# Top-32 attention with two expert layers on one core: where a step's reciprocal, two-slope pass, bias and scaling stand among the weight conversion's parts, and the order of the first loads

## The chip, the cores and the metric

The kernel runs as one program on one core of a Trainium2 chip. The metric is the device time of one execution in microseconds (us); for a set of runs it is the median. An engine works through its own queue in order, and waits on semaphores of other engines or of DMA transfers. PE is the matrix engine (PEld its weight loads), DVE the vector engine, ACT the scalar engine, POOL the general one (GpSimd), and SP the queue that issues the DMA transfers.

## What is computed

```python
scores = scale * np.matmul(q, k.transpose(0, 1, 3, 2))      # 4 batches, 8 heads, 576 x 576
kth = np.partition(scores, -32, axis=-1)[..., -32:-31]
scores = np.where(scores >= kth, scores, -1e9)
attn = np.exp(scores - scores.max(-1, keepdims=True))
attn = attn / (attn.sum(-1, keepdims=True) + 1e-9)
x = np.matmul(attn, v)                                       # regrouped to 2304 tokens x 512
h = (x @ w1) * (x @ w2) @ w3                                 # 512 -> 1024 -> 1024
x = h @ w_out                                                # 1024 -> 512
# then eight experts: P from x @ w_gate by exp and eight rounds of row and column scaling
out = sum(P[:, e:e + 1] * (np.maximum(x @ w1e[e], 0) @ w2e[e]) for e in range(8))
```

All inputs and outputs are float32. The change touches the attention alone, and beside it the conversion of the weights `w_out`, `w3`, `w1` and `w2`.

## The kernel before, in words

**Steps.** The attention is cut into 72 steps. A step `s` takes two tiles of 128 query rows against 576 keys, for two heads of one pair `p` (a pair lasts four and a half steps). The work of one step is spread over several passes of the loop at line 610. In pass `s` the program issues:

- `st_topk(s)` on DVE: the 32 largest of each row by four rounds of MAX8 (line 220) with MATCH_REPLACE8 between (line 226), for both tiles; it fills `tkv`.
- `st_rec(s - 2)` on DVE: the reciprocal of the row sums `rden` (line 254), between the two first MAX8 of `st_topk(s)`.
- `st_over(s - 1)` on ACT, twice: the two-slope pass over `s_sb` with the 32nd value from `tkv` (line 233). `st_bias(s - 1)` on POOL: `nbias` from `tkv` (line 238).
- `st_norm(s - 2)` on POOL, twice: `e_sb` times the reciprocal (line 260).
- `st_scores(s + 1, 0)` and later `(s + 1, 1)`: four matmuls (line 197) and ACT's copy to `s_sb` (line 201).
- `st_exp(s - 1, 0)` and later `(s - 1, 1)` on ACT: the exponential with `nbias` (line 245), which adds up `rden`; behind the second, `eps` is added to `rden` (line 248).
- `st_trans(s - 2, 0)` and `(s - 2, 1)`: PE transposes `e_sb` (line 266), ACT copies to `et` (line 269); then `st_av(s - 2)`: PE times `v` (line 299) and ACT's copy to `xT` (line 303).

The program is written in this order and stands so in each engine's queue; there is no scheduler. Between these parts stand pieces of a pair's preparation (`prep_split`, `prep_group`, `prep_swap`: `k` and `q` are split in two parts, transposed by PE, and the transposed `k` in `kst0` is copied with its halves exchanged to `kst1` by DMA, line 158) and matmuls that were put on a list to be filled in (`run_fill`).

**The weight conversion.** In passes 0 to 21 forty blocks of 128 x 512 weights are converted as well. `cv_run` issues ACT's part at the end of a pass: two activations (lines 350 and 351, which write `ca` in `G` and `cb`), and a third (355) for blocks of `w_out`. DVE's parts, `c1` (358), `c2` (362) and `c3` (372), wait on a list, `dve_q`; `st_topk` of the next pass takes one from it behind each pair of MAX8 and each pair of MATCH_REPLACE8 (`dve_slot`), so seven times a step. `c3` also issues POOL's addition (line 375, or 377 for `w1` and `w2`, for `w_out` with 370 ahead of it) and the load of a later block (323, on SP's queue). For `w1` and `w2`, ACT's rounding (333) and POOL's remainder (334) follow at `cv_flush`. A step with two blocks thus has 13 instructions of the search and up to six parts of the conversion on DVE.

Since `st_bias` and `st_norm` are called behind `st_topk`, they stand in POOL's queue behind the additions that `st_topk` has issued through `dve_slot`.

**The first loads.** Ahead of the loop, lines 573 to 594 load the first pair's `k`, `q` and `v`, the first block of `w_out`, split and transpose `k` and `q`, load the second pair's `k` and `q`, two more blocks, the second pair's `v`, exchange the halves of `kst` by two transfers of 288 KB, and issue the first scores.

Behind the attention (from about 925 us) stands the expert part, whose code the change doesn't touch.

Of the kernel before, what the change touches and what calls it, by code (L numbers as in the profile page):

```python
# [7 lines left out]
F32 = mybir.dt.float32  # L8
F32R = mybir.dt.float32r
U16 = mybir.dt.uint16  # L10
U32 = mybir.dt.uint32
AF = mybir.ActivationFunctionType
# [5 lines left out]
def kernel(  # L18
# [14 lines left out]
    nc = tc.nc  # L33
    B, H, S, D = q.shape
# [10 lines left out]
    S4 = R * 128  # L45
# [26 lines left out]
    ap1 = att.enter_context(tc.tile_pool(name="att", bufs=1, side="right"))  # L72
# [21 lines left out]
    def load_pair(p):  # L94
        b, hp = divmod(p, HP)
        for nm, src in (("k", k), ("q", q)):
            t = ap1.tile([128, 2 * R + 1, D], F32, name=f"{nm}n", tag=f"{nm}n", bufs=1)
            nc.sync.dma_start(
                t[:, 0:2 * R].rearrange("p (h r) d -> p h (r d)", h=2),
                src[b, 2 * hp:2 * hp + 2, 0:S4, :].rearrange("h (p r) d -> p h (r d)", r=R))  # L100
            for i in range(2):
                nc.sync.dma_start(t[64 * i:64 * i + 64, 2 * R], src[b, 2 * hp + i, S4:S, :])
            nat[nm, p] = t

    def load_v(p):
        b, hp = divmod(p, HP)
        t = vn_t[p % 2]
        for i in range(2):
            nc.sync.dma_start(t[:, R * i:R * i + R, 0:D],
                              v[b, 2 * hp + i, 0:S4, :].rearrange("(p r) d -> p r d", r=R))  # L110
        for i in range(2):
            nc.sync.dma_start(t[64:128, 2 * R + i, 0:D], v[b, 2 * hp + i, S4:S, :])

    kst = {}
    split = {}

    def copy(dst, src, eng):
        if eng is None:
            nc.scalar.activation(dst, src, AF.Copy)
        else:  # L120
            eng.tensor_copy(dst, src)

    def prep_split(p, nm, eng=nc.gpsimd):
        src = nat.pop((nm, p))
        hl = ap1.tile([128, 2 * R + 1, 2, D], F32R, name=f"{nm}hl", tag=f"{nm}hl")
        nc.scalar.activation(hl[:, :, 0, :], src, AF.Copy)
        eng.tensor_tensor(hl[:, :, 1, :], src, hl[:, :, 0, :].bitcast(F32), ALU.subtract)
        split[nm, p] = hl

    def prep_group(p, nm, g, eng=None):  # L130

        hl = split[nm, p]
        pt = mps.tile([128, 512], F32, name="pt", tag="mm")
        chunks = list(range(R * g, R * g + R)) if g < 2 else [2 * R]
        for j, c in enumerate(chunks):
            src = hl[:, c].rearrange("p a d -> p (a d)")
            nc.tensor.transpose(pt[:, 128 * j:128 * j + 128], src.bitcast(F32), ident)  # L137
        if nm == "q":
            dst = qst_t[p % 2]
            if g < 2:  # L140
                copy(dst[:, S4 * g:S4 * g + S4], pt, eng)
            else:
                copy(dst[:, 2 * S4:2 * S4 + 64], pt[:, 0:64], eng)
                copy(dst[:, 2 * S4 + 192:2 * S4 + 256], pt[:, 64:128], eng)
        else:
            if (p, 0) not in kst:
                kst[p, 0] = ap1.tile([128, 2, S], F32R, name="kst0", tag="kst0", bufs=2)
            dst = kst[p, 0]
            if g < 2:
                copy(dst[:, g, 0:S4], pt, eng)  # L150
            else:
                copy(dst[:, :, S4:S], pt[:, 0:128].rearrange("p (h r) -> p h r", h=2), eng)

    def prep_swap(p):

        kst[p, 1] = ap1.tile([128, 2, S], F32R, name="kst1", tag="kst1", bufs=2)
        for i in range(2):
            nc.sync.dma_start(kst[p, 1][64 * i:64 * i + 64].bitcast(F32),
                              kst[p, 0][64 - 64 * i:128 - 64 * i].bitcast(F32))

    def prep_list(p):
        ops = [lambda: prep_split(p, "k"), lambda: prep_split(p, "q")]
# [19 lines left out]
    eps = const.tile([128, 1], F32, name="eps")  # L182
# [23 lines left out]
    def dve_slot(n=1):  # L206
        for _ in range(n):
            if dve_q:
                fn = dve_q.pop(0)
                if fn is not None:  # L210
                    fn()

    def st_topk(st, between):

        s = [s_sb[st][:, j] for j in range(2)]
        a = [ap1.tile([128, S], F32, name=f"tk{j}", tag=f"tk{j}") for j in range(2)]
        vt = ap1.tile([128, 2, TOPK], F32, name="tkv", tag="tkv", bufs=3)
        for r in range(TOPK // 8):
            for j in range(2):
                nc.vector.max(vt[:, j, 8 * r:8 * r + 8], a[j] if r else s[j])  # L220
                if between:
                    between.pop(0)()
            dve_slot()
            if r < TOPK // 8 - 1:
                for j in range(2):
                    nc.vector.match_replace(a[j], vt[:, j, 8 * r:8 * r + 8], a[j] if r else s[j], -3.0e38)  # L226
                dve_slot()
        tkv[st] = vt

    def st_over(st, j):  # L230

        x = s_sb[st][:, j]
        nc.scalar.activation(x, x, AF.Prelu, bias=tkv[st][:, j, TOPK - 1:TOPK], scale=-1.0, alpha=2.0 ** -100)

    def st_bias(st):
        nbias[st] = ap1.tile([128, 2], F32, name="nbias", tag="nbias", bufs=2)
        vt = tkv.pop(st)
        nc.gpsimd.tensor_tensor(nbias[st], vt[:, :, TOPK - 1], vt[:, :, 0], ALU.subtract)
# [13 lines left out]
    def st_rec(st):  # L252
        rd = rden[st]
        nc.vector.reciprocal(rd, rd)

    def st_norm(st):
        rd = rden.pop(st)
        for j in range(2):
            e = e_sb[st][:, j]
            nc.gpsimd.tensor_scalar(e, e, rd[:, j:j + 1], 1.0, op0=ALU.mult, op1=ALU.mult)  # L260
# [197 lines left out]
    def moe1_pool():  # L458
        m1p["cvx2"].close()
        m1p["p"] = wab.enter_context(tc.tile_pool(name="moe1", bufs=1, side="left"))  # L460
        m1p["x2"] = keep
# [109 lines left out]
        fn()  # L571
        cpos[0] = n + 1
    load_pair(0)
    load_v(0)
    cvs = cv_list()
    cpos = [0]
    NCA = len(cvs) - FC
    cvs[0][1]()
    prep_split(0, "k", nc.vector)
    prep_split(0, "q", nc.vector)  # L580
    load_pair(1)
    cvs[1][1]()
    cvs[2][1]()
    load_v(1)
    for g in range(3):
        prep_group(0, "k", g, nc.vector if g == 1 else None)
    prep_swap(0)
    prep_group(0, "q", 0, nc.vector)
    prep_group(0, "q", 1)
    st_scores(0, 0)  # L590
    st_scores(0, 1)
# [18 lines left out]
    for s in range(NS + 6):  # L610
        for fn in loads.get(s, []):
            fn()
        now[0] = s
        if s >= marks[0] and "p" not in m1p and cpos[0] == len(cvs) and not dve_q and not cv_post:
            moe1_pool()
        fill.extend(later_q.pop(s, []))
        left = min([m for m in marks if m > s], default=s) - s
        if left and s + left == marks[-1]:
            left += 0.6
        per = (sum(c for c, _ in fill) / left if "p" in m1p and left else 0 if "p" in m1p else 5500.0) / 4  # L620
        pl = list(prep.get(s, []))

        def some_prep(k):
            for _ in range(k):
                if pl:
                    pl.pop(0)()

        old, new, nxt = 0 <= s - 2 < NS, 0 <= s - 1 < NS, s + 1 < NS
        if s < NS:
            st_topk(s, [lambda: st_rec(s - 2)] if old else [])  # L630
        elif old:
            st_rec(s - 2)
        if new:
            st_over(s - 1, 0)
            st_over(s - 1, 1)
            st_bias(s - 1)
        if old:
            st_norm(s - 2)
        if nxt:
            st_scores(s + 1, 0)  # L640
        if new:
            st_exp(s - 1, 0)
        while pend and "p" in m1p:
            items = moe1_list(pend.pop(0))
            items.pop(0)[1]()
            fill.extend(items)
        some_prep(1)
        run_fill(per)
        if old:
            st_trans(s - 2, 0)  # L650
        if new:
            st_exp(s - 1, 1)
        if nxt:
            st_scores(s + 1, 1)
        some_prep(1)
        run_fill(0.5 * per)
        if old:
            st_trans(s - 2, 1)
        if 0 < s and cpos[0] < len(cvs):
            run_cv()  # L660
        cv_flush()
        some_prep(1)
        run_fill(1.5 * per)
        if old:
            st_av(s - 2)
        if s in pdone and pdone[s] % HP == HP - 1:
            pend.append(pdone[s] // HP)
            if s == marks[-1]:
                run_fill(1e9)
        some_prep(9)  # L670
        run_fill(per)
        if cpos[0] < len(cvs):
            run_cv()
# [166 lines left out]
    hs = {}  # L840
# [196 lines left out]
```

## Time and profile before

| | us |
|---|---|
| median of 3 runs | 2562.97 (2562.9 to 2563.13) |
| profiled execution | 2561.71 |
| span of the profile | 2559.8 |
| PE busy | 2296.9 (90% of the span) |
| DVE busy | 1956.3 (76%) |
| POOL busy | 1335.9 (52%) |
| ACT busy | 1258.3 (49%) |

The profile is that of one execution. Busy times are summed over the whole span, so they say little about one stage: the conversion lies in the first 440 us, the attention goes on alone with the first expert layer until about 925 us, and the rest is the second. A view of a stage (busy time of each engine between two times, with the mean TensorE clock that was granted), a list of who waited for whom, and the instructions in order of time are what is read here. In the list of waits a row names the instruction that waited, what released it, the total, the number of waits and the longest.

### The profile page before, as it was taken

How to read it: one execution, taken by the hardware profiler on the slowest of the kernel's cores; microseconds unless marked ns; L12 is line 12 of the kernel's file. 1: busy time of each engine (PE TensorE's matmuls, PEld its weight loads, DVE VectorE, ACT ScalarE, POOL GpSimd, SP SyncE). 2: the span in 40 equal slices, each digit the busy share in tenths (PEclk: the TensorE clock that was granted, in tenths of full speed). 3: DMA queues.
4: the chain of work that ended last, by engine and by line, in shares of the span. 5: the costliest groups of instructions: out<-in, count | busy, mean ns of one | idle time of the engine just before them, and what ended most of it. 6: DMA issues, size and time to landing. Idle time of an engine off the chain costs nothing.

```text
span 2559.8 us, 37892 instructions
## 1 busy us (share of the span) xinstructions
PE 2296.9 (90%) x13061; PEld 2010.3 (79%) x13061; DVE 1956.3 (76%) x3560; ACT 1258.3 (49%) x2724; POOL 1335.9 (52%) x1377
## 2 busy tenths in 40 slices
PE   3456654999999999999999999999999999999999
PEld 2333434988878978888999998888888899999998
DVE  6756577999999933788777777877777777777776
ACT  4555466777777743444444344434444443444432
POOL 3322234333324221658666667866666666666664
PEclk9777777999999999999999999999999999999999
DMA  4212221111111012222222223222222232222222
GB/s 121 77 55 72 60 73 36 42 39 39 46 47 28 21 40 91 89 71 78 66 67 66 67 73 109 66 67 71 71 66 66 66 91 71 71 66 67 66 67 58
DMA packets 172848, 166.59 MB, mean 65 GB/s; under 512 B 19312, under 2 KB 137072, under 8 KB 172656
## 3 DMA queue, kind: packets, MB, share of 16 engines
q1 hardware_dynamic: 172656, 164.17, 21.7%
q8 instruction: 103, 1.69, 0.3%
q14 instruction: 89, 0.73, 0.1%
HBM read 145.24 MB, written 9.44 MB: 60 GB/s over the span
## 4 chain that ended last, share of the span: by engine, by line
PE 73%; DVE 6%; ACT 3%; POOL 2%; issue 1%; DMA 0%; SPq 0%; POOLq 0%; DVEq 0%; ACTq 0%
PE y L924 30%; PE l1ps L857 26%; PE abps L491 7%; PE x2ps L509 4%; PE xps L299 2%; PE sps L197 2%; DVE tk L226 1%; DVE tkv L220 1%; PE tps L266 1%; ACT et L269 1%; ACT e_sb L245 1%; PE pt L137 1%; DVE hl L881 1%; ACT s_sb L201 1%; DVE ws L714 0%
## 5 line engine op out<-in xcount | busy, mean ns | idle before, releaser
L721 POOL TENSOR_TENSOR wal<-ws,wah 128x256 fp32r<-128x256 f32 x665 | 554.0, 840 | 481.6 <-ACT wah L720 471.8
L937 DVE SCALAR_TENSOR_TENSOR acc<-y,P,acc 128x512 f32<-128x512 f32 x540 | 402.3, 745 | 218.1 <-PE y L924 217.3
L720 ACT ACTIVATE wah<-ws 128x256 fp32r<-128x256 f32 x672 | 276.4, 413 | 523.6 <-PE l1ps L857 516.1
L924 PE MATMUL y<-wbh,hh 128*128 128x512 f32 x1152 | 456.4, 396 | 3.2 <-ACT hh L878 3.2
L924 PE MATMUL y<-wbl,hh 128*128 128x512 f32 x1152 | 454.6, 395 | 0.0
L924 PE MATMUL y<-wbh,hl 128*128 128x512 f32 x1152 | 449.2, 390 | 2.2 <-DVE hl L881 1.7
L714 DVE TENSOR_TENSOR ws<-ws 128x256 f32<-128x256 f32 x384 | 316.0, 824 | 2.6 <-DMA ws<-in_moe_w_dram 2.5
L857 PE MATMUL l1ps<-xo0h,wah 128*128 128x384 f32 x896 | 304.5, 340 | 0.0
L220 DVE MAX8 tkv<-tk 128x8 f32<-128x576 f32 x432 | 304.2, 745 | 0.0
L857 PE MATMUL l1ps<-xo0h,wal 128*128 128x384 f32 x896 | 302.7, 338 | 0.0
L857 PE MATMUL l1ps<-xo0l,wah 128*128 128x384 f32 x896 | 302.5, 338 | 0.0
L924 PEld LDWEIGHTS y<-wbl,hh 128*128 128x128 f32 x1152 | 216.1, 188 | 52.6
L878 ACT ACTIVATE hh<-u 128x384 fp32r<-128x384 f32 x192 | 100.9, 525 | 299.3 <-DVE u L870 299.3
L924 PEld LDWEIGHTS y<-wbh,hl 128*128 128x128 f32 x1152 | 216.8, 188 | 30.4 <-DVE hl L881 5.9
L729 POOL TENSOR_TENSOR wbl<-ws,wbh 128x1024 fp32r<-128x1024 f32 x96 | 231.9, 2415 | 12.4 <-ACT wbh L728 4.5
L924 PEld LDWEIGHTS y<-wbh,hh 128*128 128x128 f32 x1152 | 216.6, 188 | 27.7 <-ACT hh L878 4.9
L266 PE MATMUL tps<-ident,e_sb 128*128 128x128 f32 x576 | 101.3, 305 | 136.5 <-POOL e_sb L260 125.6
L226 DVE MATCH_REPLACE8 tk<-tkv,tk 128x576 f32<-128x576 f32 x288 | 211.3, 740 | 0.0
L266 PEld LDWEIGHTS tps<-ident,e_sb 128*128 128x128 f32 x576 | 76.3, 157 | 168.5 <-POOL e_sb L260 137.2
L857 PEld LDWEIGHTS l1ps<-xo0l,wah 128*128 128x128 f32 x896 | 169.2, 189 | 16.4
L857 PEld LDWEIGHTS l1ps<-xo0h,wah 128*128 128x128 f32 x896 | 168.9, 189 | 15.8 <-DVE hl L881 0.6
L500 POOL TENSOR_TENSOR G<-a_sb 128x256 f32<-128x256 f32 (+1 forms) x64 | 52.3, 816 | 233.5 <-ACT a_sb L496 218.7
(146 smaller groups left out, 5063.4 us busy)
## 6 DMA issues: line engine op xcount, KB each, us to landing
ws<-in_moe_w_dram SPq DMA_DIRECT2D x384, 128.0 KB, 2.3
ws<-in_moe_w_dram SPq DMA_DIRECT2D x96, 512.0 KB, 3.5
raw<-in_moe_w_dram SPq DMA_DIRECT2D x32, 512.0 KB, 3.8
kst<-kst SPq DMA_DIRECT2D x32, 288.0 KB, 4.0
xr<-x2s SPq DMA_DIRECT2D x12, 384.0 KB, 3.8
xr<-x2s SPq DMA_DIRECT2D x6, 768.0 KB, 4.6
kn<-in_k_dram SPq DMA_DIRECT2D x16, 256.0 KB, 2.7
qn<-in_q_dram SPq DMA_DIRECT2D x16, 256.0 KB, 2.8
```

The source lines that it names most:

```text
L220: nc.vector.max(vt[:, j, 8 * r:8 * r + 8], a[j] if r else s[j])
L226: nc.vector.match_replace(a[j], vt[:, j, 8 * r:8 * r + 8], a[j] if r else s[j], -3.0e38)
L266: nc.tensor.transpose(ps[:, 128 * c:128 * c + 128], e[:, 128 * c:128 * c + 128], ident)
L491: nc.tensor.matmul(ps[:, 0:n], lhs[:, c, fs], rhs[:, c, 0:n], start=(c == 0 and j == 0), stop=(c == KD - 1 and j == 2))
L509: nc.tensor.matmul(ps[:, 0:n], W[:, f, 128 * c:128 * c + 128], G[:, f, 0:n], start=(f == 0), stop=(f == FC - 1))
L714: nc.vector.tensor_tensor(st[:, dst], st[:, x], st[:, y], op)
L720: nc.scalar.activation(hi, st[:, slot], AF.Copy)
L721: eng.tensor_tensor(lo, st[:, slot], hi.bitcast(F32), ALU.subtract)
L729: nc.gpsimd.tensor_tensor(lo, st, hi.bitcast(F32), ALU.subtract)
L857: nc.tensor.matmul(ps[:, 0:TH], lhs[:, c], rhs[:, slot, c], start=(k_ == 0), stop=(k_ == 3 * KH - 1))
L924: nc.tensor.matmul(ps, lhs[:, m, h, o:o + 128], rhs[:, m], start=(k_ == 0), stop=(k_ == 5))
L937: nc.vector.scalar_tensor_tensor(a, ps, P[:, t, e:e + 1], a, op0=ALU.mult, op1=ALU.add)
```

## The change: what it does

In a pass, the reciprocal of step `s - 2`, the two-slope pass and the bias of step `s - 1`, and the scaling of step `s - 2` become one function, `head`, which `st_topk` calls behind its first MAX8, that is ahead of every `dve_slot`. DVE's own order stays as it was in the loop (the reciprocal stood there before), and so does ACT's (nothing of the conversion was issued to ACT inside `st_topk`). What changes is POOL's queue in passes 1 to 22.

Here is POOL's queue before, in passes 6 and 7. `nbias` and `e_sb` with `rden` are the bias and the scaling, `G` and `w3r` the additions of the conversion, `w1l` a remainder.

```order
L377 TENSOR_TENSOR G_88<-G_88 128x512
L375 TENSOR_TENSOR w3r_791<-G_88 128x512
L238 TENSOR_TENSOR nbias_797<-tkv_658 128x2
L260 TENSOR_SCALAR e_sb_701<-e_sb_701,rden_702 128x576 x2
L334 TENSOR_TENSOR w1l_90<-G_88,w1h_89 128x512
L375 TENSOR_TENSOR w3r_918<-G_88 128x512
L375 TENSOR_TENSOR w3r_931<-G_88 128x512
L238 TENSOR_TENSOR nbias_937<-tkv_766 128x2
L260 TENSOR_SCALAR e_sb_808<-e_sb_808,rden_809 128x576 x2
```

And the same two passes now:

```order
L239 TENSOR_TENSOR nbias_776<-tkv_663 128x2
L261 TENSOR_SCALAR e_sb_706<-e_sb_706,rden_707 128x576 x2
L378 TENSOR_TENSOR G_88<-G_88 128x512
L376 TENSOR_TENSOR w3r_802<-G_88 128x512
L335 TENSOR_TENSOR w1l_90<-G_88,w1h_89 128x512
L239 TENSOR_TENSOR nbias_915<-tkv_771 128x2
L261 TENSOR_SCALAR e_sb_813<-e_sb_813,rden_814 128x576 x2
L376 TENSOR_TENSOR w3r_929<-G_88 128x512
L376 TENSOR_TENSOR w3r_942<-G_88 128x512
```

The bias and the scaling of a pass went ahead of that pass's two additions, and a remainder now stands ahead of the next pass's bias.

The second part is the start. Behind the loads of the first `k` and `q`, the queue of SP (`kn`, `qn`, `vn` are the loads of `k`, `q`, `v`) was:

```order
L109 DMA vn0_91<-in_v_dram 128x256 x2
L112 DMA vn0_91<-in_v_dram 64x64 x2
L323 DMA raw_124<-in_moe_w_out_dram 128x2048
L98 DMA kn_132<-in_k_dram 128x2x256
L102 DMA kn_132<-in_k_dram 64x64 x2
L98 DMA qn_136<-in_q_dram 128x2x256
L102 DMA qn_136<-in_q_dram 64x64 x2
L323 DMA raw_140<-in_moe_w_out_dram 128x2048
L323 DMA raw_142<-in_moe_w_out_dram 128x2048
L109 DMA vn1_92<-in_v_dram 128x256 x2
L112 DMA vn1_92<-in_v_dram 64x64 x2
L158 DMA kst1_164<-kst0_153 64x1152 x2
```

and it is now:

```order
L324 DMA raw_120<-in_moe_w_out_dram 128x2048
L159 DMA kst1_133<-kst0_131 64x512 x2
L159 DMA kst1_133<-kst0_131 64x2x64 x2
L159 DMA kst1_133<-kst0_131 64x512 x2
L98 DMA kn_158<-in_k_dram 128x2x256
L102 DMA kn_158<-in_k_dram 64x64 x2
L98 DMA qn_162<-in_q_dram 128x2x256
L102 DMA qn_162<-in_q_dram 64x64 x2
L109 DMA vn0_91<-in_v_dram 128x256 x2
L112 DMA vn0_91<-in_v_dram 64x64 x2
L324 DMA raw_170<-in_moe_w_out_dram 128x2048
```

The exchange of `kst`'s halves moved ahead of the second pair's loads and was cut in three parts; the first `v` and the second and third block of `w_out` (`raw`) moved behind it. On ACT an activation of `eps` on itself stands ahead of everything, and with it the load of ACT's function table; ACT's split of `q` moved behind its copy of `k`'s first group; one copy went from ACT to DVE and one from DVE to ACT.

```diff
-    def prep_swap(p):
+    def prep_swap(p, hs=slice(0, 2), ts=slice(0, S)):
...
         for i in range(2):
-            nc.sync.dma_start(kst[p, 1][64 * i:64 * i + 64].bitcast(F32),
-                              kst[p, 0][64 - 64 * i:128 - 64 * i].bitcast(F32))
+            nc.sync.dma_start(kst[p, 1][64 * i:64 * i + 64, hs, ts].bitcast(F32),
+                              kst[p, 0][64 - 64 * i:128 - 64 * i, hs, ts].bitcast(F32))
...
     load_pair(0)
-    load_v(0)
...
     cvs[0][1]()
+    nc.scalar.activation(eps, eps, AF.Copy)
     prep_split(0, "k", nc.vector)
+    prep_group(0, "k", 0)
+    prep_swap(0, slice(0, 1), slice(0, S4))
     prep_split(0, "q", nc.vector)
+    prep_group(0, "k", 2, nc.vector)
+    prep_swap(0, slice(0, 2), slice(S4, S))
+    prep_group(0, "q", 0)
+    prep_group(0, "k", 1, nc.vector)
+    prep_swap(0, slice(1, 2), slice(0, S4))
     load_pair(1)
+    load_v(0)
     cvs[1][1]()
     cvs[2][1]()
     load_v(1)
-    for g in range(3):
-        prep_group(0, "k", g, nc.vector if g == 1 else None)
-    prep_swap(0)
-    prep_group(0, "q", 0, nc.vector)
     prep_group(0, "q", 1)
...
+        def head():
+            if old:
+                st_rec(s - 2)
+            if new:
+                st_over(s - 1, 0)
+                st_over(s - 1, 1)
+                st_bias(s - 1)
+            if old:
+                st_norm(s - 2)
+
         if s < NS:
-            st_topk(s, [lambda: st_rec(s - 2)] if old else [])
-        elif old:
-            st_rec(s - 2)
-        if new:
-            st_over(s - 1, 0)
-            st_over(s - 1, 1)
-            st_bias(s - 1)
-        if old:
-            st_norm(s - 2)
+            st_topk(s, [head])
+        else:
+            head()
```

More of the change, by code (lines that the diff above doesn't have):

```diff
@@ L152, in prep_group @@
                 copy(dst[:, :, S4:S], pt[:, 0:128].rearrange("p (h r) -> p h r", h=2), eng)
-    def prep_swap(p):
-        kst[p, 1] = ap1.tile([128, 2, S], F32R, name="kst1", tag="kst1", bufs=2)
+    def prep_swap(p, hs=slice(0, 2), ts=slice(0, S)):
+        if (p, 1) not in kst:
+            kst[p, 1] = ap1.tile([128, 2, S], F32R, name="kst1", tag="kst1", bufs=2)
         for i in range(2):
-            nc.sync.dma_start(kst[p, 1][64 * i:64 * i + 64].bitcast(F32),
-                              kst[p, 0][64 - 64 * i:128 - 64 * i].bitcast(F32))
+            nc.sync.dma_start(kst[p, 1][64 * i:64 * i + 64, hs, ts].bitcast(F32),
+                              kst[p, 0][64 - 64 * i:128 - 64 * i, hs, ts].bitcast(F32))
     def prep_list(p):
```

## The prediction

> **What bounds the kernel now.** I read the stage view first: the busy time of each engine between two times, with counts. Its columns are the stretch and its length, then PE, PEld, DVE, ACT and POOL busy, the granted TensorE clock and two DMA figures.
>
> ```profile
> 94.28:331.13 236.85, 135.29 (x669) 86.97 (x668) 144.62 (x297) 116.30 (x226) 57.49 (x64) 0.76 0.20 60
> 331.13:355.17 24.04, 18.41 (x132) 11.94 (x130) 21.26 (x44) 20.20 (x44) 11.01 (x12) 0.93 0.32 103
> 355.17:429.33 74.16, 25.43 (x161) 21.31 (x162) 55.72 (x110) 37.50 (x73) 25.53 (x27) 0.68 0.16 48
> 439.55:449.25 9.70, 9.07 (x81) 8.36 (x80) 9.70 (x22) 8.05 (x19) 2.43 (x5) 0.98 0.25 63
> ```
>
> The first row holds steps 5 to 15 (eleven, the reciprocals at line 254 count them), the second two steps with little conversion, the third steps 18 to 21 with `w2`, the last one step behind the conversion. There DVE is busy for all of its 9.70 us: the search bounds the attention alone. In the conversion a step takes 236.85 / 11 = 21.5 us, of which DVE works 144.62 / 11 = 13.1. What DVE waits for between 46.91 and 439.55 us (steps 2 to 22) is the next view, its list of waits:
>
> ```profile
> DVE rden L254 <- ACT rden L248: 77.5, 18, 8.2
> DVE G L358 <- ACT cb L351: 41.2, 20, 3.9
> DVE tkv L220 <- ACT s_sb L201: 6.1, 18, 0.6
> ```
>
> Together 124.8 us, all on ACT: for the row sums of the step before last, and for ACT's part of a weight block. Why ACT is late is seen in the instructions in order of time around the border of steps 10 and 11:
>
> ```profile
> 199.74 0.74 DVE L220 MAX8 tkv<-s_sb 128x8 f32<-128x576 f32 x1
> ...
> 218.09 1.26 POOL L375 TENSOR_TENSOR w3r<-G 128x512 f32<-128x512 f32 x1 [4.99 <-DVE G L372]
> 219.20 0.74 DVE L220 MAX8 tkv<-s_sb 128x8 f32<-128x576 f32 x1
> 219.31 0.20 POOL L238 TENSOR_TENSOR nbias<-tkv 128x2 f32<-128x2 f32 x1
> 219.48 1.47 POOL L260 TENSOR_SCALAR e_sb<-e_sb,rden 128x576 f32<-128x576 f32 x2
> 219.54 0.77 ACT L245 ACTIVATE e_sb<-s_sb,nbias 128x576 f32<-128x576 f32 x1 [4.28 <-POOL nbias L238]
> ...
> 223.14 0.29 ACT L248 ACTIVATE rden<-rden,eps 128x2 f32<-128x2 f32 x1
> ...
> 223.53 0.17 DVE L254 RECIPROCAL rden<-rden 128x2 f32<-128x2 f32 x1 [3.60 <-ACT rden L248]
> ```
>
> Step 10's first MAX8 starts at 199.74, so step 9's `tkv` was complete then. Its bias is formed at 219.31, 19.6 us later, as soon as POOL is through with the addition of step 10's second block, which itself waited 4.99 us for `c3`, a part at the end of DVE's step. The exponential follows at once, the row sums at 223.14, and DVE has stood since its first MAX8. So a circle runs once a step: DVE's last part of the conversion, POOL's addition, bias, two exponentials, reciprocal, DVE again. What ACT waits for in steps 5 to 15:
>
> ```profile
> ACT e_sb L245 <- POOL nbias L238: 66.5, 11, 8.3
> ACT et L269 <- PE tps L267: 28.9, 17, 4.9
> ACT xT L303 <- PE xps L299: 19.8, 9, 5.0
> ACT W L452 <- PE wps L450: 4.2, 4, 1.6
> ```
>
> **The change part by part.** *Bias and scaling on POOL.* The bias needs only `tkv` of step `s - 1`, ready as step `s` begins; the scaling needs the reciprocal, which stands behind the first MAX8, 0.7 us in. In front of the two additions they cost these 0.20 + 1.47 us, but an addition waits for a `c3` that stands behind four MAX8, two MATCH_REPLACE8 and two other parts, some 5 us into a step by the 0.74 of a MAX8, so they are hidden; were that cover gone, it would be 1.7 us a step. The remainder at line 334 now stands ahead of the next bias and waits for ACT's rounding; that is a wait of the same step, over before the next begins unless ACT is late by more than DVE's conversion allows. No DMA moves with the head, and DVE's and ACT's queues keep their order in the loop.
>
> With the bias at a step's start, ACT can form the row sums (3.6 us from 219.54 to 223.14, behind the two-slope pass and one copy) by the middle of a step; DVE asks for them at the next step's start. The 77.5 us go, and so do the 6.1, which follow the same waits by 0.3 us each. The 41.2 us go as far as ACT now ends its step within DVE's 13.1 us, and that is the open size. ACT's work is 116.30 / 11 = 10.6 us a step; with its waits for PE, (28.9 + 19.8 + 4.2) / 11 = 4.8, that makes 15.4, more than 13.1. These waits are inflated by the clock: PE stands idle while the bias is late, and starts cold. Two matmuls of the same kind from step 10, behind an idle PE and 7 us on:
>
> ```profile
> 207.75 2.08 PE L450 MATMUL wps<-wo,w3t 128*128 128x512 f32 x2 [2.10 <-ACT w3t L442]
> ...
> 214.46 1.02 PE L450 MATMUL wps<-wo,w3t 128*128 128x512 f32 x2
> ```
>
> The granted clock is 0.76 over steps 5 to 15, and 0.93 in the next row, where the bias was hardly late. If the clock goes to that, most of these waits halve, ACT needs 10.6 + 2.4 = 13.0 us, and DVE is the bound again, with ACT just under it. A late ACT is also buffered: its block parts are due 1.5 and some 6 us into the next step. I take back 10 us for steps in which ACT still comes late, half a microsecond for each of 20. Ends: nothing back (ACT always under 13.1), or ACT at 15.4 with the clock as it is, 11 x (15.4 - 13.1) = 25 us back. I am nearer to the first since 0.93 is the row without the late bias.
>
> Steps 18 to 21 hold 74.16 - 55.72 = 18.4 of the 124.8 us; ACT's own work there is 37.50, so they fall to DVE's 55.7.
>
> *The start.* The rows, ACT, then SP, then DVE, and two of the DMA issues in the first 30 us (KB each, us to landing):
>
> ```profile
> 5.05 1.28 ACT L126 ACT_TABLE_LOAD   x1 [5.05 <-DMA kn<-in_k_dram]
> ```
>
> ```profile
> 5.18 1.06 SPq L109 DMA_DIRECT2D vn<-in_v_dram  x2
> ...
> 7.52 0.58 SPq L323 DMA_DIRECT2D raw<-in_moe_w_out_dram  x1
> 8.20 0.38 SPq L98 DMA_DIRECT2D kn<-in_k_dram  x1
> ...
> 11.59 1.06 SPq L323 DMA_DIRECT2D raw<-in_moe_w_out_dram  x2
> ```
>
> ```profile
> 9.88 0.69 DVE L121 CAST kst<-pt 128x512 fp32r<-128x512 f32 x1 [1.40 <-PE pt L137]
> ...
> 26.09 0.73 DVE L358 SCALAR_TENSOR_TENSOR G<-G,cb 128x512 uint16<-128x512 f32 x1 [0.62 <-ACT cb L351]
> ...
> 29.84 0.79 DVE L358 SCALAR_TENSOR_TENSOR G<-G,cb 128x512 uint16<-128x512 f32 x1
> ```
>
> ```profile
> raw<-in_moe_w_out_dram SPq DMA_DIRECT2D x3, 512.0 KB, 4.3
> kst<-kst SPq DMA_DIRECT2D x2, 288.0 KB, 5.1
> ```
>
> The table load now runs before `k` has landed: 1.28 us earlier on. The last copy into `kst0`, at 9.88 before, now comes behind the split and the transposes of `q`; with the 1.28 off I put its end at 12.4. The last exchange is then issued at 12.5 to 13.7 and lands by 18.7 at the larger transfer's 5.1. The second score tile, ACT's copy and its first block's part add about 3 us, so DVE's first `c1` could go from 26.09 to some 21. But the second block's load now stands behind the exchange, the second pair's loads (8.20 to 11.59, 3.4 us) and the first `v` (5.18 to 7.52, 2.3 us): it is issued at 13.7 + 3.4 + 2.3 = 19.4, lands 4.3 us later at 24 with its issue, and two activations put the second `c1` at 25.5 instead of 29.84. So the start gains 4.3 us; the load of the second block hides the rest of the earlier scores. Ends: 2 us if that load lands 2 us later still, 7 if it doesn't decide. The activation of `eps` itself lies under the wait for `k`.
>
> **The sum**, against the profiled execution's 2561.71 us (its span of 2559.8 and 1.9 around it): 124.8 - 10 + 4.3 = 119.1 less, 2442.6. The median of the runs is 1.26 above the profiled execution: 2443.9, rounded to 2444. Behind 440 us nothing changes but the time at which it begins.
>
> **The rivals.** *ACT and PE stay the bound.* For it: 15.4 us a step without the bias's wait, in the rows above. Against it: the clock of 0.93. It gives 124.8 - 25 + 4.3 = 104 less: 2459.
>
> *DVE and POOL get in each other's way.* POOL's scaling now runs in a step's first 2.5 us, beside `c1`, which reads two operands from SBUF. One of DVE's `c1` in the start overlapped an addition on POOL:
>
> ```profile
> 30.11 1.62 POOL L375 TENSOR_TENSOR wo<-G 128x512 f32<-128x512 f32 x1
> ```
>
> DVE's at 29.84 took 0.79 us beside it, against 0.73 for the one at 26.09, when POOL was idle. By that, 20 steps lose 1.2 us, which the 10 above hold. If a `c1` had to wait for a whole scaling instruction (1.47 / 2 = 0.73), 20 steps would lose 15 us: 2459 again. The Trainium skill (page "SBUF — State Buffer", section "SBUF: two separate sides") says that a DVE instruction with two SBUF inputs and a GpSimd instruction that reads SBUF take the shared ports as a lock, so that the later one blocks for the whole of the other. By that rule the price would be the larger one; the 0.06 us of the row don't bear it out for DVE.
>
> *The change does not reach the cause.* If the exponential had been late for something else than the bias's place, only the start would gain: 2558.7, within 0.2% (5.1 us, about what a measurement of this kernel can tell from no change). Against it stands 219.31 right behind 218.09 + 1.26 with its input ready for 19 us.
>
> *Slower: the clock behind the conversion.* In the present trace TensorE gets 0.98 in the step at 439.55, after a stage at 0.68. From there 2120 us are left, in which PE is busy nearly always. If a PE that is kept warm from 60 us on were granted less later, the loss would be in proportion: 119 us are given back at 0.98 / (1 + 119 / 2120) = 0.93, and below that the kernel is slower; at 0.92 it is 2444 + 2120 x (0.98 / 0.92 - 1) = 2582. Nothing in the trace shows such a debt.
>
> **How the numbers follow.** Forecast 0.70, ACT and PE 0.14, DVE and POOL 0.06, the cause not reached 0.05, clock 0.03, and 0.02 for a start that loses some us, with the rest of the gain kept or shrunk. The range reaches from no stall at all and the best start, 124.8 + 7 = 132 less, 2431, to the first two rivals with a start of 2 and a little beyond, 2464. What lies outside has 0.10 at least. Faster by over 0.2%: the first three and a part of the rest, 0.92; within: 0.05; slower: 0.03.
>
> **What would show it.** Right: DVE's waits at line 254 near zero in steps 2 to 22 and the bias right at a step's first MAX8; steps 5 to 15 at 13 to 14 us with a granted clock above 0.9; the step that starts at 439.55 now starting near 320; second `c1` at about 25.5. Wrong in size: waits of `c1` for line 351 that stay at 2 us a step (ACT and PE), or `c1` taking more than 0.8 us (ports). Wrong in kind: line 254 still waiting for line 248.

## The result and the profile after

The changed kernel takes 2445.02 us (median of 4 runs, 2443.9 to 2446.91) against 2562.93 of the kernel before, measured in the same session: a ratio of 0.9542, 95% interval 0.9526 to 0.9559. The profiled execution has a span of 2442.0 us, 117.8 less than the 2559.8 of before, and three points on VectorE's (DVE's) queue share it out. Step 2's reciprocal stands at 42.34 us where it stood at 47.71: 5.4. From there to step 23's reciprocal, the first behind the conversion, it takes 281.01 us in place of 392.64: 111.6. The rest, 2118.65 us, was 2119.45: 0.8. Line numbers of the changed kernel are one higher than before at most places (the reciprocal L255, the bias L239, the scaling L261, the parts `c1` L359, `c2` L363, `c3` L373).

First the stage view again: stretch and length, then busy time and count of TensorE (PE), its weight loads, DVE, ScalarE (ACT) and POOL, then the granted clock, the DMA share and GB/s. The rows are steps 5 to 15, the four steps with `w2`, and one step behind the conversion.

```profile
77.50:233.80 156.30, 116.42 (x629) 73.13 (x630) 146.13 (x299) 108.57 (x215) 62.70 (x64) 0.89 0.30 91
...
258.21:312.84 54.63, 34.30 (x175) 26.67 (x174) 54.63 (x109) 38.88 (x77) 25.61 (x26) 0.60 0.22 65
322.55:332.25 9.70, 9.53 (x81) 8.62 (x81) 9.70 (x22) 8.04 (x18) 2.29 (x5) 0.91 0.26 63
```

Eleven steps take 156.30 us instead of 236.85, with the same DVE work in them (146.13 and 144.62): 14.2 us a step. The granted clock went from 0.76 to 0.89. In the `w2` steps DVE never idles: 54.63 of 54.63. What DVE still waits for from 41.54 to 322.55 us:

```profile
DVE G L359 <- ACT cb L352: 9.0, 5, 2.6
DVE rden L255 <- ACT rden L249: 3.1, 2, 2.1
DVE tkv L221 <- ACT s_sb L202: 1.1, 3, 0.4
```

13.2 us in place of 124.8, and 124.8 - 13.2 = 111.6 is the whole of the time by which steps 2 to 22 became shorter. The mechanism can be read off the beginning of step 5 (start, length, engine, line, operation, count, and in brackets the idle time before it with its releaser):

```profile
77.64 0.74 DVE L221 MAX8 tkv<-s_sb 128x8 f32<-128x576 f32 x1
77.80 0.20 POOL L239 TENSOR_TENSOR nbias<-tkv 128x2 f32<-128x2 f32 x1 [1.51 <-DVE tkv L221]
78.30 0.14 DVE L255 RECIPROCAL rden<-rden 128x2 f32<-128x2 f32 x1
...
78.61 1.90 POOL L261 TENSOR_SCALAR e_sb<-e_sb,rden 128x576 f32<-128x576 f32 x2 [0.62 <-DVE rden L255]
78.97 0.76 ACT L246 ACTIVATE e_sb<-s_sb,nbias 128x576 f32<-128x576 f32 x1
79.02 0.91 DVE L359 SCALAR_TENSOR_TENSOR G<-G,cb 128x512 uint16<-128x512 f32 x1
```

Here the bias waits for its own input, the search's last MAX8, and is done 0.4 us into the step; POOL is free for it. The reciprocal follows the first MAX8 without a wait. It is not so in every step: in 13 of the 21 steps from 2 to 22 the bias starts 1.4 to 9.1 us behind the first MAX8, because a remainder, or POOL's part of the split of a pair's `k` and `q`, stands ahead of it on POOL. ACT mostly comes to the exponential later than that: from 41.54 to 322.55 us it waits 3.4 us for the bias, where it waited 115.3 us from 46.91 to 439.55 before. What ACT waits for in steps 5 to 15:

```profile
ACT xT L304 <- PE xps L300: 19.0, 8, 6.1
ACT et L270 <- PE tps L268: 18.9, 7, 4.9
ACT G L351 <- POOL w1l L335: 5.4, 3, 4.7
ACT W L453 <- PE wps L451: 3.8, 3, 1.6
```

The bias's 66.5 us are gone from this list; the waits for PE are 19.0 + 18.9 + 3.8 = 41.7, where they were 52.9. The start, on the queues of SP and DVE (two views, the DMA issues first):

```profile
8.35 5.24 SPq L159 DMA_DIRECT2D kst<-kst  x6
...
19.56 1.06 SPq L324 DMA_DIRECT2D raw<-in_moe_w_out_dram  x2
```

```profile
11.75 0.69 DVE L121 CAST kst<-pt 128x512 fp32r<-128x512 f32 x1 [1.86 <-PE pt L137]
...
18.09 0.73 DVE L359 SCALAR_TENSOR_TENSOR G<-G,cb 128x512 uint16<-128x512 f32 x1 [0.60 <-ACT cb L352]
...
24.50 0.74 DVE L359 SCALAR_TENSOR_TENSOR G<-G,cb 128x512 uint16<-128x512 f32 x1 [2.59 <-ACT cb L352]
...
42.34 0.14 DVE L255 RECIPROCAL rden<-rden 128x2 f32<-128x2 f32 x1
```

The second of those `c1` waits for ACT's two activations of the second block, the first of which waits for the block's load:

```profile
23.08 0.75 ACT L351 ACTIVATE G<-raw,cbias 128x512 f32<-128x512 uint16 x1 [4.33 <-DMA raw<-in_moe_w_out_dram]
```

The first `c1` comes 8 us earlier (18.09 for 26.09), the second only 5.34 (24.50 for 29.84), after a wait of 2.59 us for ACT, which waits for the second block's load, issued at 19.56. Step 2 moved by as much as the second `c1`.

### The profile page after: what moved, and what is told of

Read it like the earlier page. It is cut to its first block, busy times and chain, and to the rows that moved or that the text cites. A ratio compares the mean times of both kernels' runs of the same rounds, so it can differ in the third digit from the quotient of the medians.

```text
span 2442.0 us, 37866 instructions
## 1 busy us (share of the span) xinstructions
PE 2288.3 (94%) x13061; PEld 2002.0 (82%) x13061; DVE 1958.9 (80%) x3560; ACT 1256.2 (51%) x2725; POOL 1343.2 (55%) x1377
## 3 DMA queue, kind: packets, MB, share of 16 engines
q1 hardware_dynamic: 173104, 164.17, 22.4%
## 4 chain that ended last, share of the span: by engine, by line
PE 80%; DVE 11%; ACT 5%; POOL 2%; issue 2%; DMA 1%; SPq 0%; POOLq 0%; DVEq 0%; ACTq 0%
PE y L933 31%; PE l1ps L866 27%; PE abps L492 8%; PE x2ps L510 4%; DVE tkv L221 4%; DVE tk L227 3%; PE xps L300 3%; PE sps L198 2%; PE tps L267 2%; PE wps L451 1%; DVE G L359 1%; PE pt L137 1%; ACT e_sb L246 1%; ACT et L270 1%; ACT s_sb L202 1%
## 5 line engine op out<-in xcount | busy, mean ns | idle before, releaser
L730 POOL TENSOR_TENSOR wal<-ws,wah 128x256 fp32r<-128x256 f32 x665 | 553.9, 840 | 482.7 <-ACT wah L729 471.7
L866 PEld LDWEIGHTS l1ps<-xo0h,wal 128*128 128x128 f32 x896 | 168.7, 188 | 0.0
L879 DVE TENSOR_TENSOR u<-l1ps,u 128x384 f32<-128x384 f32 x288 | 157.2, 546 | 4.8 <-PE l1ps L866 3.0
```

Source lines behind the costliest of these rows:

```text
L730: eng.tensor_tensor(lo, st[:, slot], hi.bitcast(F32), ALU.subtract)
L866: nc.tensor.matmul(ps[:, 0:TH], lhs[:, c], rhs[:, slot, c], start=(k_ == 0), stop=(k_ == 3 * KH - 1))
L879: nc.vector.tensor_tensor(t[nm], ps, t[x], ALU.add)
```

## The experiments

My theory was the prediction's: the head's place on POOL carries nearly all of it, the start some 5 us, and the 13 us of waits left are ACT held by PE. Each run below is a separate kernel; ratios are to the kernel before, with a 95% interval.

**The head alone, with the old start.** All of the diff up to the loop is taken back.

```diff
-    prep_group(0, "k", 0)
-    prep_swap(0, slice(0, 1), slice(0, S4))
...
+    for g in range(3):
+        prep_group(0, "k", g, nc.vector if g == 1 else None)
+    prep_swap(0)
```

> Only the head moves; the first loads stay as before. Theory (two independent parts; the start is worth the 5.4 us by which step 2 came earlier, 47.71 to 42.34): 2445.0 + 5.4 = 2450.4. Rival (the later steps would have swallowed the earlier start): 2445.

Measured: 2452.24 us, ratio 0.9563 (0.9547 to 0.9579). Step 2's reciprocal is back at 48.24, and DVE's waits behind it are 9.5 + 4.2 + 0.7 = 14.4 us. The head is worth 111 us, and what remains of the change, some 7 us by these medians, is the start.

**The start alone, with the old loop.**

```diff
-            st_topk(s, [head])
-        else:
-            head()
+            st_topk(s, [lambda: st_rec(s - 2)] if old else [])
+        elif old:
+            st_rec(s - 2)
+        if new:
+            st_over(s - 1, 0)
+            st_over(s - 1, 1)
+            st_bias(s - 1)
+        if old:
+            st_norm(s - 2)
```

> Only the first loads change; the loop stays as before. Theory: 2562.9 - 5.4 = 2557.5, with DVE's waits for the row sums and the block parts at 124.8 us as before. Rival (the old circle swallows an earlier start): 2562.9.

Measured: 2558.91 us, ratio 0.9982 (0.9973 to 0.9991). The second `c1` stands at 26.14, step 2's reciprocal at 43.97, and DVE's waits are those of before (77.3, 43.4 and 6.1 us). So the start alone gives 4.5 us (2563.41 of the kernel before in that session, less 2558.91), and the two parts add to 115.7 of the whole 117.9 us. The 2 us between are within the spread of the runs.

**The bias moved, the scaling not.**

```diff
             if new:
                 st_over(s - 1, 0)
                 st_over(s - 1, 1)
                 st_bias(s - 1)
-            if old:
-                st_norm(s - 2)
...
+        if old:
+            st_norm(s - 2)
```

> The bias goes ahead of the conversion's additions on POOL, the scaling stays behind them. Theory (the circle has two links, since ACT's copy of the first transposed tile, which waits for the scaling, stands ahead of the second exponential on ACT): the scaling ends 13.3 us into a step as before, the row sums come 16 us into it, DVE still waits 2 to 3 us a step at the reciprocal and 1 to 2 for the block parts, so most of the 112 us of the loop is lost: 2500 to 2540. Rival (the bias is the cause alone): 2445 to 2450.

This kernel and the next have the new start. Measured: 2538.97 us, ratio 0.9907 (0.9892 to 0.9922), which is 19.9 us less than with the start alone (2558.91). DVE's waits from 42 to 440 us, then the instructions around a step's border with the releasers in brackets:

```profile
DVE rden L255 <- ACT rden L249: 56.6, 18, 3.5
DVE G L359 <- ACT cb L352: 41.9, 19, 3.9
DVE tkv L221 <- ACT s_sb L202: 6.2, 18, 0.6
```

```profile
199.27 0.77 ACT L246 ACTIVATE e_sb<-s_sb,nbias 128x576 f32<-128x576 f32 x1
...
202.17 1.26 POOL L376 TENSOR_TENSOR w3r<-G 128x512 f32<-128x512 f32 x1 [4.58 <-DVE G L373]
...
203.41 1.47 POOL L261 TENSOR_SCALAR e_sb<-e_sb,rden 128x576 f32<-128x576 f32 x2
204.21 0.71 PEld L267 LDWEIGHTS tps<-ident,e_sb 128*128 128x128 f32 x4 [4.02 <-POOL e_sb L261]
...
205.58 0.70 ACT L270 ACTIVATE et<-tps 128x640 f32<-128x640 f32 x1 [4.47 <-PE tps L268]
206.18 0.77 ACT L246 ACTIVATE e_sb<-s_sb,nbias 128x576 f32<-128x576 f32 x1
...
207.46 0.17 DVE L255 RECIPROCAL rden<-rden 128x2 f32<-128x2 f32 x1 [3.45 <-ACT rden L249]
```

The first exponential is early now (199.27). But the scaling of the step before stands behind the addition, which waits 4.58 us for `c3`; PE's transposes wait for the scaling, ACT's copy `et` for the transposes, and the second exponential stands behind that copy on ACT's queue. The reciprocal is late again by the same circle, closed through another link.

**The scaling moved, the bias not.**

```diff
-            if new:
-                st_over(s - 1, 0)
-                st_over(s - 1, 1)
-                st_bias(s - 1)
...
+        if new:
+            st_over(s - 1, 0)
+            st_over(s - 1, 1)
+            st_bias(s - 1)
```

> The scaling goes ahead of the additions, the bias (and the two-slope pass) stays behind them. Theory: the first exponential still starts 13.5 us into a step, the row sums come 16 us into it, DVE's waits at the reciprocal fall from 3.6 to some 2 us a step: 2515 to 2550. Rival (the scaling is the cause alone): 2445 to 2455.

Measured: 2551.3 us, ratio 0.9955 (0.994 to 0.9969). That is just above the theory's range, and 7.6 us less than with the start alone. ACT waits 65.6 us for the bias from 90 to 320 us, and DVE 65.2 for the row sums from 42 to 440. So 19.9 us for one half of the head, 7.6 for the other, 113.9 for both: each link alone leaves the circle closed. The stretch from step 2's reciprocal to step 23's shows it without the rest: 394.77 us with the start alone, 372.33 with the bias moved, 379.85 with the scaling moved, 281.01 with both. With the scaling moved alone some of that is lost again behind the conversion, where no addition stands in the way: steps 23 to 73 take 489.6 us for the changed kernel's 482.7, and ACT waits 13.0 us there for the bias (2.1 in the changed kernel), which stands behind the scaling on POOL.

**The first conversion part of a step one slot later.** It was meant to take `c1` out of the way of POOL's scaling and remainders.

```diff
-            dve_slot()
+            if r:
+                dve_slot()
```

> The changed kernel, but the conversion's parts start one place later in a step: none is issued behind the first pair of MAX8, so the first c1 stands behind the first two MATCH_REPLACE8, about 3 us into a step instead of 1.4, when POOL's scaling and the late remainders are over. Theory (c1's 37 runs take 32.7 us instead of 27.5 since POOL holds something that c1 needs; and DVE's 9.0 us of waits for ACT's block parts are a matter of 1 to 2 us each): c1's mean falls from 0.88 back to 0.75 us, most of the 9.0 us of waits go, 2445 - 8 = 2437. Rival (c1 is longer for another reason, or the last c3, now at a step's end, makes POOL and ACT late): c1 stays at 0.85 to 0.9, 2445 to 2450.

Measured: 2445.45 us, ratio 0.954 (0.9527 to 0.9553): nothing gained, a miss. The cost that I wanted to remove was real, and most of it stayed. Here are the 37 `c1` of steps 2 to 22 (busy us, mean ns | idle before) in the kernel before, the changed one, and this one, whose lines are one higher:

```profile
L358 DVE SCALAR_TENSOR_TENSOR G<-G,cb 128x512 uint16<-128x512 f32 x37 | 27.5, 742 | 41.2 <-ACT cb L351 41.2
```

```profile
L359 DVE SCALAR_TENSOR_TENSOR G<-G,cb 128x512 uint16<-128x512 f32 x37 | 32.7, 883 | 9.0 <-ACT cb L352 9.0
```

```profile
L360 DVE SCALAR_TENSOR_TENSOR G<-G,cb 128x512 uint16<-128x512 f32 x37 | 30.5, 825 | 4.8 <-ACT cb L353 4.8
```

The change added 5.2 us to `c1`; this edit took 2.2 back. In the changed kernel seven `c1` start beside the scaling, and four beside a remainder. With the edit three still pay beside the scaling (0.78 to 0.88 us each), and three, in the `w2` steps, beside a remainder (1.63 to 1.67). DVE's waits went from 13.2 to 10.2 + 4.8 + 1.1 = 16.1. Where the parts stand a slot later, the block that they belong to is done later, and the waits took back what `c1` gave. That sequence is argued; the two sums are measured.

**The second block's load ahead of the second pair's.** It was the load that held the second `c1`.

```diff
+    cvs[1][1]()
     load_pair(1)
     load_v(0)
-    cvs[1][1]()
     cvs[2][1]()
```

> The changed kernel, but the second block of w_out is loaded ahead of the second pair's loads and the first v. Theory (that load decides when the second c1 runs, which waits 2.6 us for ACT): the second c1 moves from 24.5 to 21.9 us, with no wait, 2445.0 - 2.6 = 2442.4. Rival (the second pair's loads, 0.6 us later, are due as well, or the steps behind swallow it): 2445.

Measured: 2444.28 us, ratio 0.9538 (0.9525 to 0.9551). The second `c1` moved to 22.63 and did not wait; step 2's reciprocal stands at 40.53, 1.8 us earlier. At step 9's reciprocal the lead had gone (132.13 and 132.44), and step 23's reciprocal stands at 323.41 for 323.35. The gain went into steps that ACT and PE hold; as the second `c1` of the other kernels with the new start stands anywhere from 24.50 to 26.14, a difference of this size is near what single profiles can tell, and I don't lean on it.

**Fifty-six of the 64 matmuls of `w3 w_out` left out.** They are the filler that PE runs between a step's transposes and scores. The product is not formed, so the output is not the reference's; the rest of the kernel runs as it was.

```diff
-        nc.tensor.matmul(wps[i], w3t[i][:, j], wo[:, j], start=(j == 0), stop=(j == FC - 1))
         if j == FC - 1:
+            nc.tensor.matmul(wps[i], w3t[i][:, j], wo[:, j], start=True, stop=True)
```

> The changed kernel with 56 of the 64 matmuls of w3 by w_out left out (each output block is formed from the last of its eight terms alone); ACT's copies and all orders stay. Theory (what is left of DVE's waits, 13.2 us between steps 2 and 22, is ACT being held up by PE in steps with many of these matmuls): the 13.2 us fall under 4, 2434 to 2437. Rival (the rest comes from late loads or from POOL): 2445, waits as they were.

Measured: 2431.76 us, ratio 0.949 (0.9477 to 0.9503). DVE has no wait at all from 38 to 330 us; its stage row between the reciprocals of steps 2 and 23, and the changed kernel's:

```profile
43.51:309.20 265.69, 159.82 (x1005) 127.01 (x1005) 265.69 (x548) 207.40 (x411) 134.27 (x132) 0.76 0.30 94
```

```profile
42.34:323.35 281.01, 197.39 (x1116) 136.10 (x1116) 267.80 (x549) 207.63 (x411) 133.24 (x132) 0.81 0.29 89
```

ACT's work is the same to 0.3 us; 37.6 us of PE's are gone, and DVE is busy for every one of 265.69 us. What was left of DVE's waits, 281.01 - 267.80 = 13.2 us, was ACT held by PE. It was not POOL: in this kernel ACT waits 22.0 us for POOL's remainders of `w1` in the same stretch, and DVE still waits for nothing. The granted clock is 0.76, lower than the changed kernel's 0.81, and did no harm here: PE is busy for 159.82 of 265.69 us.

**`c3` off DVE for all blocks.** ACT scales the exponent word and POOL multiplies, as they do for `w_out`.

```diff
-        off = key[0] == "o"
+        off = True
```

> The changed kernel, with c3 taken off DVE for all 40 blocks as w_out's blocks have it: ACT scales the remainder first (one activation of 0.67 us more a block) and POOL multiplies. DVE is rid of 32 x 0.6 = 19 us, ACT gets 21 us. Theory (in steps 5 to 15 ACT with its waits for PE is just under DVE's time, so that ACT becomes the bound there; only the w2 steps gain, 8 x 0.6 = 5 us): DVE's waits for ACT grow from 13 to 25 us or more, 2438 to 2450. Rival (DVE alone is the bound now): 2426.

Measured: 2447.04 us, ratio 0.9549 (0.9536 to 0.9562). DVE's work from 40 to 320 us falls from 266.79 to 249.98 and its waits rise to 22.3 + 4.7 + 1.5 + 1.5 = 30.0, nearly all for ACT, whose work rises from 206.66 to 223.57. Steps 2 to 17 take 223.2 us for the changed kernel's 216.7, so neither DVE nor ACT can give to the other there; the four `w2` steps gain, 49.33 for 54.63.

**The filler behind everything else of a pass.** In the conversion the four places where a pass may issue filler become one, at its end.

```diff
+        f0, f1, f2, f3 = (1, 0.5, 1.5, 1) if "p" in m1p else (0, 0, 0, 4)
...
-        run_fill(1.5 * per)
+        run_fill(f2 * per)
```

> The changed kernel with the early w3.w_out work of a conversion pass issued behind the pass's other PE work instead of spread between its transposes and scores. Theory (what is left of VectorE's waits, 13.2 us, is ScalarE standing behind a few of TensorE's filler groups; the kernel without most of the fillers had no such wait): with the fillers last, the transposes reach ScalarE sooner, most of the 13.2 us goes, and step 23's reciprocal comes near 313; some 2435 us, 2432 to 2440. Rival (the fillers cost PE time wherever they stand, and hold the next step's transposes or scores just as long): the waits stay at 10 to 15 us, no change within 0.2%, about 2445 us.

Measured: 2456.44 us, ratio 0.9582 (0.9569 to 0.9595): 11 us slower than the change, and worse than the rival. ACT's waits in the same 156.30 us as above (here some ten steps), and the instructions in one of the late steps:

```profile
ACT W L453 <- PE wps L451: 21.7, 6, 5.2
ACT w3t L443 <- PE pt L442: 17.8, 8, 4.7
ACT xT L304 <- PE xps L300: 4.9, 6, 1.2
...
ACT et L270 <- PE tps L268: 0.8, 1, 0.8
```

```profile
138.07 3.70 PE L451 MATMUL wps<-wo,w3t 128*128 128x512 f32 x8 [0.69 <-ACT w3t L443]
141.60 0.60 PE L442 MATMUL pt<-ident,w3r 128*128 128x128 f32 x4
142.24 0.60 ACT L443 ACTIVATE w3t<-pt 128x512 f32<-128x512 f32 x1 [4.23 <-PE pt L442]
142.74 0.75 ACT L351 ACTIVATE G<-raw,cbias 128x512 f32<-128x512 uint16 x1
...
143.38 0.75 ACT L352 ACTIVATE cb<-raw,cbias 128x512 f32<-128x512 uint16 x1
...
144.23 0.76 DVE L359 SCALAR_TENSOR_TENSOR G<-G,cb 128x512 uint16<-128x512 f32 x1 [2.58 <-ACT cb L352]
```

The waits for `et` and `xT` went from 37.9 to 5.7 us, as expected. In their place ACT waits for the filler's own products: its copy at 142.24 stands behind eight filler matmuls and a transpose, and the next block's two activations behind that copy, with `c1` behind them. DVE's wait for ACT's block part became 22.4 us. The filler's ACT instructions are in the same queue as everything else, so in one lump they hold what stands behind the lump: ACT waits 21.7 + 17.8 = 39.5 us for the filler's matmuls and transposes, where it waits 3.8 + 0.3 = 4.1 when they are spread.

**`c3` off DVE in the `w2` steps alone.** There DVE never idles and ACT had 38.88 us of work in 54.63 (the 34.3 in the expectation is PE's column).

```diff
-        off = key[0] == "o"
+        off = key[0] in ("o", 1)
```

> The changed kernel with VectorE's fourth conversion instruction, c3, taken off VectorE in the four steps that convert w2 alone, and given to ScalarE and POOL there. Theory (in those steps VectorE never idles and is the bound, while ScalarE has 34.3 us of work in 54.6 us): each of the four steps loses VectorE's 1.2 us or so of c3, some 4 to 5 us in all; 2440 us, 2438 to 2443. Rival (POOL, which already carries the remainders there, is late with them, and VectorE waits for it instead, or the next stage swallows the gain): 2444 to 2448 us.

Measured: 2440.62 us, ratio 0.9521 (0.9508 to 0.9534). The four `w2` steps take 49.11 us, from the reciprocal at 260.97 to that at 310.08. The changed kernel takes 54.63 for them, from 259.01 to 313.64, and so do the kernels with the load ahead and with few filler matmuls (54.60 and 54.63); the one with `c3` off for all blocks took 49.33. So the stage gives 5.5 us, and the medians differ by 4.4. The interval overlaps that of the changed kernel, so the run times alone don't settle that the whole is faster; that the stage is shorter, the profiles do.

**The last two and the load together.**

> The three edits together: fillers last, c3 of w2 off VectorE, and the raw copy's part first at the start (which alone brought step 2 forward by 1.8 us and lost it again in the steps that ScalarE and TensorE held). Theory (the gains add once VectorE waits for nothing: 8 to 10 from the fillers, 4 to 5 from w2, 1.8 from the start): some 2430 us, 2426 to 2436. Rival (one engine's limit stands right behind another's, so that the gains don't add): 2438 to 2445 us.

Measured: 2445.89 us, ratio 0.9543 (0.953 to 0.9556). That misses the theory and lies just above the rival's range: the gains don't add. Step 2's reciprocal stands at 39.88 us, 2.5 earlier than in the changed kernel; steps 2 to 17 take 224.3 us for 216.7 (225.0 with the filler last alone), and the `w2` steps 51.56 for 54.63. So the lump of filler takes back what the start and the `w2` steps give, and it costs in the `w2` steps too, which take 49.11 us without it. The lowest median of a kernel that forms the whole product is the one above.

## Why the prediction was right

It forecast 2444.0 and 2445.02 was measured. The mechanism was right, and the terms were near: 114.8 us forecast for steps 2 to 22 and 111.6 measured, 4.3 and 5.4 for the start, nothing and 0.8 for the rest. That the sum came out within 1 us or so is partly luck, as these misses go against each other and the size of the first had a wrong reason. Of the prediction's signs, the row at the reciprocal and step 23's place came about as it said. The others did not quite: the bias stands at a step's first MAX8 in 8 of 21 steps, steps 5 to 15 took 14.2 us each for 13 to 14, the clock was 0.89 and not above 0.9, and `c1` took 0.883 us, over the 0.8 that was to speak for the ports. Point by point:

**The circle.** Right. The waits went as the bias and the scaling moved, the row at the reciprocal from 77.5 to 3.1 us, and step 23 starts at 323.35 (forecast: near 320). The text was too narrow in one respect: it drew the circle through the bias and the exponentials only. The bias alone brought 19.9 us; the scaling's link, through PE's transposes and ACT's copy, carries the same lateness. The forecast came out because the change moves both.

**Ten microseconds taken back for ACT and PE.** 13.2 measured, and all of it is this cause, as the kernel with few filler matmuls shows. But the reason given for the size failed: the waits of ACT for PE were to halve with the clock, from 4.8 us a step to 2.4, and they went to 41.7 / 11 = 3.8, although the clock rose to 0.89. They cost little because ACT has room in many of the steps in which they fall. Steps 5, 6 and 10 to 12 take 12.8 to 13.0 us, DVE's own work, with 17 of the 41.7 us of these waits in them; steps 8, 9 and 14 to 16 take 14.4 to 17.2. What sets the second group apart was not tried. An average per step was the wrong tool.

**The start.** 4.3 us forecast; 5.4 in the profile, 4.5 by the kernel with the start alone, and 7 by the kernel without it. The deciding load was named rightly: its issue was put at 19.4 and is at 19.56, and when it went ahead the wait of the second `c1` vanished. The last copy into `kst0` was put at 12.4 and ends at 12.44. The first `c1` was put at 21 and comes at 18.09, without effect.

**DVE and POOL.** Undersized, and laid to the wrong instruction. The one row of before said 0.06 us for a `c1` beside POOL; 37 of them cost 5.2 us in all. The scaling, for which the rival asked 15 us, made 1.3 of it: seven `c1` started beside it, 0.39 to 0.48 us behind the start of its first instruction, and found at most 0.36 us of that instruction left. The other 4.0 us are four `c1` that started up to 0.24 us behind a remainder and took 1.62 to 1.77 us. Here a step of the prediction failed: it held a remainder to be over before the next step begins, unless ACT is late. In the changed kernel a remainder stands in the way of the bias in 11 of the 21 steps from 2 to 22; in steps 19 to 21, where DVE waits for nothing, it starts within 0.1 us of the step's first MAX8. The forecast hardly suffered, as ACT waited only 3.4 us for these biases.

The row of before was misread, too. The `c1` at 29.84 began when POOL's instruction ahead of the addition had 0.19 us left, so it had little to pay; the addition, at 30.11, began beside a running `c1` and took 1.62 us, for 1.26 in the row at 218.09. I read only DVE's side of that row. DVE's busy time as a whole did not grow (267.8 in both), so the sum did not notice: `c2` fell from 18.7 to 17.6 and the first pairs of MAX8 from 31.4 to 30.8, and where the rest of the 5.2 went was not followed up.

**The clock behind the conversion.** No debt: the last 2119 us are within 1 us of before, at a granted clock of 0.99 in both.

## What to carry to other kernels

When an engine waits once a step, follow the chain back until it closes on the engine itself; then look for every link of the circle that stands in a queue behind work which it doesn't need, and move all of them, since one alone gives back little. A producer that is late on average matters only in the steps in which it has no room, so count those steps and not the mean. And before filler work is moved out of the way, look at who empties its results: if it is an engine with an in-order queue, spread filler can be cheaper than filler in a lump, as it was here by 11 us.

## What the hardware showed that I had not expected

When `c1`, a DVE instruction with two tensor inputs, starts beside a running POOL instruction, it pays for what is left of that one; and when it is POOL's that starts later, POOL's pays. In the changed kernel, a step of the `w2` stage (the first row is the second of two remainders) and the start of step 5, each row one instruction:

```profile
272.66 1.28 POOL L335 TENSOR_TENSOR w2l<-G,w2h 128x512 fp32r<-128x512 f32 x1
272.77 1.75 DVE L359 SCALAR_TENSOR_TENSOR G<-G,cb 128x512 uint16<-128x512 f32 x1
273.89 0.66 POOL L239 TENSOR_TENSOR nbias<-tkv 128x2 f32<-128x2 f32 x1
```

```profile
78.61 0.74 POOL L261 TENSOR_SCALAR e_sb<-e_sb,rden 128x576 f32<-128x576 f32 x1 [0.62 <-DVE rden L255]
79.02 0.91 DVE L359 SCALAR_TENSOR_TENSOR G<-G,cb 128x512 uint16<-128x512 f32 x1
79.33 1.18 POOL L261 TENSOR_SCALAR e_sb<-e_sb,rden 128x576 f32<-128x576 f32 x1
```

The remainder, of two tensor inputs, ends at 273.94, 1.17 us behind the start of `c1`; `c1` took 1.75 us, 1.01 more than its usual 0.74. The scaling's first instruction, of one tensor input, ends at 79.35, 0.33 us behind the start of `c1`, which took 0.17 more. In both cases the extra is 0.16 us less than what was left. It is 0.12 to 0.16 us less for all 11 `c1` of the changed kernel's steps 2 to 22 that found 0.27 us or more of a scaling or a remainder left (up to 1.18). So the price goes by how late in POOL's instruction `c1` starts, and no difference between the two kinds is seen. What the 0.15 us or so are, no run here shows. POOL pays by the same measure: the bias at 273.89 had 0.63 us of `c1` ahead of it and took 0.46 over its usual 0.20; the scaling's second instruction had 0.60 ahead of it and took 0.44 over its 0.74.

The Trainium skill (page "SBUF — State Buffer", section "SBUF: two separate sides") states a lock on shared ports, in which the later of two such instructions waits for the whole of the other. The rows of the remainder and of the scaling agree with that but for the 0.15 us. The rival's 15 us had stood for a `c1` that meets a whole scaling instruction; the seven that met one found the last 0.27 to 0.36 us of it.
